# A decode kernel (sliding-window attention beside a SwiGLU block): SyncE's wait for the output put behind the block, two loads put ahead of the branches into it

## The chip, the cores and the metric

The kernel runs on one core of a Trainium2 chip. Its time is the device time of one execution in microseconds (us); the figure used is the median of several executions. The core has five engines: TensorE (PE, with its weight loads shown as PEld), VectorE (DVE), ScalarE (ACT), GpSimd (POOL) and SyncE (SP), which computes nothing and issues transfers here. Each engine works through its own list of instructions, in order. They meet only at semaphores: an instruction can wait until a semaphore has reached a value, and can raise one when it is done. A transfer (DMA) is issued by an engine, is then carried out by 16 DMA engines that all queues share, and raises its semaphore by 16 when it has landed.

## What is computed

The reference, cut to what matters (B = 4, one query token, D = 512, 32 query heads on 8 key heads, Dh = 128, a window W of the last 4096 of 16384 cached keys, F = 1792; all bf16):

```python
x = A_x
xn = layernorm(x)
q = (xn @ wq)                                  # per head
k, v = k_cache[:, :, Sk - W:], v_cache[:, :, Sk - W:]
scores = einsum("bhqd,bhkd->bhqk", q, k) * Dh ** -0.5
o = einsum("bhqk,bhkd->bhqd", softmax(scores), v)
ffn = (silu(xn @ w_gate) * (xn @ w_up)) @ w_down
return x + o.reshape(B, 1, Hq * Dh) @ wo + ffn
```

## The kernel before

The kernel is written engine by engine inside one `nc.Block()` (L171): five functions, one for each engine, are the lists of instructions that the engines branch into when the block begins. The order on every engine is the one written there; no planner moves anything. When the block ends, all engines go through a barrier: each drains and raises a common semaphore, POOL collects the four others and then releases all of them. These instructions carry the block's line, L171. A barrier of the same kind stands ahead of the kernel's first instruction and carries L500, the line at which the program is made.

SP issues all the large loads, in one queue: W_Q (L231), the first two blocks of K (`load_k`, L217), W_gate and W_up (L234, L235), then by turns a block of V (`load_v`, L221) and a block of K, 16 of each in all, then W_down (L240), the last block of V in halves (L225) and W_O in four groups of 16, 10, 4 and 2 of its 32 parts (L229; `WO_CUTS`, L120). K and V have two buffers each. Before a K block is issued, SP waits for the transposes that read the buffer's former content (`s_tr`), and before a V block for the products that read the V buffer (`s_pv`). Last, SP waits for the result y (L246), issues its first half to memory (L247) and waits until both halves have landed (L248: `d_out` at 32, 16 for each half). That wait rides on SP's branch out of the block.

ACT issues the load of x (L252), which has a queue of its own, and at the end the other half of y (L267). Between them it computes: the layer norm's steps (L254 to L260), an exponential for each block of scores (L263), and one for the gate (L265). ACT does not wait for its half of the output; SP's wait covers it.

The layer norm goes from DVE (L272, the row sum, which waits for x) over ACT (L254 to L260) and PE (L359, four small transposes) back to DVE (L279, which writes xnT). PE then waits for W_Q and multiplies (L354, called from L369). In the loop over the 16 blocks, PE transposes K (L382), DVE copies the transposes out of PSUM (L294), and PE forms scores and the products with V (L354). Behind the loop come the gate and up products, the last V block, W_down, and last the products with W_O, each group of which waits for its load (L483). The product's end lets DVE copy y out of PSUM (L349), and this releases both output transfers.

POOL fills constants at the start (L175 to L210) and then goes to the block's end.

Of the kernel before, what the change touches and what calls it, by code (L numbers as in the profile page):

```python
# [10 lines left out]
def bass_parallel_sum__sliding_block_cached__swiglu_ffn__decode_kernel(  # L11
# [10 lines left out]
    out: bass.AP,  # L22
):
    B, _, D = A_x.shape
    _, HKV, Sk, Dh = A_k_cache.shape
    HQ = A_wq.shape[1] // Dh
    F = B_w_gate.shape[1]
# [25 lines left out]
    WQ = sb("wq_sb", [128, NC * HQ * Dh], BF16)  # L53
# [18 lines left out]
    X = sb("x_sb", [B, D], BF16)  # L72
# [39 lines left out]
    def sem(name):  # L112
        return nc.alloc_semaphore(name=name)
    d_x = sem("d_x")
    d_wq = sem("d_wq")
# [3 lines left out]
    d_out = sem("d_out")  # L119
# [38 lines left out]
    x_ap = A_x.rearrange("b s d -> (b s) d")  # L158
    out_ap = out.rearrange("b s (n c) -> n (b s) c", n=2)
    wq_ap = A_wq.rearrange("(p c) n -> p (c n)", c=NC)  # L160
# [6 lines left out]
    def kv_ap(cache, d):  # L167
        b0 = d % 2 * 2
        return cache[b0:b0 + 2, d // 2, Sk - W:, :].rearrange("b (q t) d -> q b (t d)", t=NT)

    with nc.Block() as block:  # L171

        @block.gpsimd
# [38 lines left out]
        @block.sync  # L212
        def _(eng):
            def load_k(d):
                if d >= 2:
                    eng.wait_ge(s_tr, 2 * NG * (d - 1))
                eng.dma_start(KB[:, d % 2 * KVN:(d % 2 + 1) * KVN], kv_ap(A_k_cache, d)).then_inc(d_k[d % 2], 16)  # L217

            def load_v(d):
                eng.wait_ge(s_pv, d + 1)  # L220
                eng.dma_start(VB[:, d % 2 * KVN:(d % 2 + 1) * KVN], kv_ap(A_v_cache, d)).then_inc(d_v[d % 2], 16)  # L221

            def load_v_half(d, h, done):
                a = d % 2 * KVN + h * HKN
                eng.dma_start(VB[:, a:a + HKN], kv_ap(A_v_cache, d)[:, :, h * HKN:(h + 1) * HKN]).then_inc(done, 16)  # L225

            def load_wo(n):
                a, b = WO_CUTS[n], WO_CUTS[n + 1]
                eng.dma_start(WO[:, a:b, :], wo_ap[:, a:b, :]).then_inc(d_wo[n], 16)  # L229

            eng.dma_start(WQ[:], wq_ap).then_inc(d_wq, 16)  # L231
            load_k(0)
            load_k(1)
            eng.dma_start(WG[:], wg_ap).then_inc(d_wg, 16)  # L234
            eng.dma_start(WU[:], wu_ap).then_inc(d_wu, 16)  # L235
            load_v(0)
            for d in range(2, ND):
                load_k(d)
                load_v(d - 1)
            eng.dma_start(WD[:], wd_ap).then_inc(d_wd, 16)  # L240
            eng.wait_ge(s_pv, ND)
            load_v_half(ND - 1, 0, d_v[1])
            load_v_half(ND - 1, 1, d_vz)
            for n in range(len(d_wo)):
                load_wo(n)
            eng.wait_ge(s_y, 1)  # L246
            eng.dma_start(out_ap[0], y[0:B, :]).then_inc(d_out, 16)  # L247
            eng.wait_ge(d_out, 32)  # L248

        @block.scalar  # L250
        def _(eng):
            eng.dma_start(X[:], x_ap).then_inc(d_x, 16)  # L252
            eng.wait_ge(s_xc, 1)
            eng.activation(xc[:], X[:], ACT.Identity, bias=st_neg[:, 0:1], scale=float(D))  # L254
            eng.drain()
            eng.activation(xsq[:], xc[:], ACT.Square, accum_out=st_sum[:, 0:1]).then_inc(s_ss, 1)
            eng.wait_ge(s_var, 1)
            eng.activation(st_std[:], st_var[:], ACT.Sqrt).then_inc(s_std, 1)
            eng.wait_ge(s_rs, 1)
            eng.activation(xn[:], xc[:], ACT.Identity, scale=st_rstd[:, 0:1]).then_inc(s_xn, 1)  # L260
            for d in range(-1, ND):
                eng.wait_ge(s_sh, d + 2)
                eng.activation(P[:, d % 2 * PS:d % 2 * PS + SN], ps_S[d % 2][:], ACT.Exp, scale=SCALE).then_inc(s_p, 1)  # L263
            eng.wait_ge(s_gt, 1)
            eng.activation(ex[:], gT.rearrange("p (t b) -> p t b", b=32)[:, :, 0:B], ACT.Exp, scale=-1.0).then_inc(s_ex, 1)  # L265
            eng.wait_ge(s_y, 1)
            eng.dma_start(out_ap[1], y[64:64 + B, :]).then_inc(d_out, 16)  # L267
# [218 lines left out]
            last.then_inc(s_acc, 1)  # L486


# [1 line left out]
_INS = ['A_x', 'A_k_cache', 'A_v_cache', 'A_wq', 'A_wo', 'B_x', 'B_w_gate', 'B_w_up', 'B_w_down']  # L490
_OUTS = [((4, 1, 512), 'bfloat16')]
# [23 lines left out]
```

## Time and profile before

| | |
|---|---|
| three runs | 197.1, 197.37 and 197.96 us; median 197.37 |
| the profiled execution, its own time | 196.87 us |
| its span, first to last instruction | 195.1 us |
| granted TensorE clock, mean | 0.991 |
| busy | PE 83%, PEld 72%, DVE 59%, ACT 9%, POOL 5% of the span |
| moved | 81.10 MB, mean 416 GB/s |

The span is what the profile shows, from the first instruction of any engine to the last. The device time is longer by what lies before and behind it. In the profile's lines, a name with a q (SPq, ACTq) is an engine's sequencer: register, branch, drain, semaphore and DMA-issuing instructions, which are not counted as busy. A line of the timeline gives start, duration, engine, line, operation, and in brackets how long the engine had been idle and what ended it. A line of a source view gives the engine, the operation, its count, the shortest, median and longest duration in ns, and the start of the first and the last. A line of the waits gives total, count and longest. A line of the table by stages gives the stage, its length, each engine's busy time with its number of instructions, the granted clock, the DMA engines' busy share and what they moved.

### The profile page before, as it was taken

What the parts mean: (1) busy time and instruction counts of PE and PEld (TensorE: products, weight loads), DVE (VectorE), ACT (ScalarE), POOL (GpSimd) and SP (SyncE); (2) the same over time, 40 slices, a digit from 0 to 9 for tenths busy, and PEclk for the clock granted to TensorE, in tenths of its full rate; (3) what the DMA queues carried; (4) which work ended last, traced back from release to release, by engine and by line L of the source; (5) the groups of instructions that cost most, each with busy time, mean ns of one, the idle gap of its engine ahead of it and who ended that gap; (6) DMA issues with size and microseconds to landing.
All of it is one profiled execution on the core that took longest, in us unless ns stands there. A gap on an engine that the chain in (4) does not pass through costs nothing.

```text
span 195.1 us, 7758 instructions
## 1 busy us (share of the span) xinstructions
PE 162.7 (83%) x3466; PEld 140.2 (72%) x3467; DVE 114.9 (59%) x250; ACT 16.6 (9%) x26; POOL 10.3 (5%) x23
## 2 busy tenths in 40 slices
PE   0127999379898989898989898989898989898995
PEld 0113898368887888788878787878787878786752
DVE  1005777237676767676767676767676767675610
ACT  5600101001010101010101010101010101010000
POOL 8930000000000000000000000000000000000000
PEclk9999999789999999999999999999999999999999
DMA  6999999999999999999999999999999999999991
GB/s 222 430 430 430 432 420 437 421 430 430 430 433 430 433 433 430 433 430 433 433 437 430 430 430 430 430 430 430 430 430 430 430 433 433 430 428 420 438 407 68
DMA packets 5934, 81.10 MB, mean 416 GB/s; under 512 B 668, under 2 KB 680, under 8 KB 936
## 3 DMA queue, kind: packets, MB, share of 16 engines
q1 hardware_dynamic: 5912, 81.01, 97.4%
q8 instruction: 5, 0.08, 0.1%
q10 hardware_dynamic: 16, 0.01, 0.0%
q14 instruction: 1, 0.01, 0.0%
HBM read 81.01 MB, written 0.00 MB: 415 GB/s over the span
## 4 chain that ended last, share of the span: by engine, by line
DMA 63%; PE 32%; issue 1%; DVE 1%; SPq 1%; DVEq 0%
DMA kbuf<-in_A_k_cache_dram 48%; PE ps_kt L382 16%; DMA wo_sb<-in_A_wo_dram 9%; PE ps_s L354 8%; DMA wq_sb<-in_A_wq_dram 6%; PE ps_o L354 5%; PE ps_acc L354 2%; PE ps_kt L354 2%; DVE kT L294 1%; SPq L225 1%; DVE kT L282 0%; SPq L229 0%; DVE y_sb L349 0%; DVE qz L285 0%; DVEq L293 0%
## 5 line engine op out<-in xcount | busy, mean ns | idle before, releaser
L294 DVE COPY kT<-ps_kt 128x1024 bf16<-128x1024 bf16 x128 | 79.5, 683 | 25.3 <-PE ps_kt L382 25.3
L382 PE MATMUL ps_kt<-ident,kbuf 128*128 128x128 bf16 x1024 | 62.8, 219 | 10.6 <-DMA kbuf<-in_A_k_cache_dram 10.6
L382 PEld LDWEIGHTS ps_kt<-ident,kbuf 128*128 128x128 bf16 x1024 | 57.3, 98 | 15.8 <-issue 15.7
L354 PE MATMUL ps_o<-p,vbuf 128*128 128x64 bf16 x1120 | 39.2, 195 | 0.0
L354 PEld LDWEIGHTS ps_o<-p,vbuf 128*128 128x128 bf16 x1120 | 36.0, 99 | 1.1
L354 PEld LDWEIGHTS ps_s<-qz,kT 128*128 128x128 bf16 x1024 | 31.7, 98 | 6.7 <-issue 3.6
L354 PE MATMUL ps_s<-qz,kT 128*128 x1024 | 34.9, 192 | 1.3
L299 DVE TENSOR_REDUCE rm<-ps_s 128x8 bf16<-128x512 f32 x17 | 11.8, 692 | 23.7 <-PE ps_s L354 23.7
L263 ACT ACTIVATE p<-ps_s 128x512 bf16<-128x512 f32 x17 | 10.1, 597 | 162.1 <-PE ps_s L354 162.1
L354 PE MATMUL ps_o<-p,ones 128*128 128x128 bf16 (+1 forms) x69 | 7.1, 225 | 4.6 <-DMA vbuf<-in_A_v_cache_dram 3.2
L354 PEld LDWEIGHTS ps_o<-p,ones 128*128 128x128 bf16 x69 | 4.6, 100 | 5.6 <-DMA vbuf<-in_A_v_cache_dram 3.4
L354 PE MATMUL ps_kt<-wq_sb,xnT 128*32 128x512 bf16 x32 | 3.4, 610 | 5.2 <-DMA wq_sb<-in_A_wq_dram 5.2
L359 PE MATMUL ps_acc<-i,xn 4*128 4x4 f32 x4 | 0.6, 254 | 7.4 <-ACT xn L260 7.4
L354 PE MATMUL ps_s<-mkc,mkr 2*128 2x512 bf16 x17 | 6.5, 385 | 0.0
L354 PE MATMUL ps_s<-dg,ones 8*128 8x512 bf16 x17 | 6.5, 385 | 0.0
L354 PEld LDWEIGHTS ps_kt<-wq_sb,xnT 128*32 128x32 bf16 x32 | 1.3, 140 | 6.8 <-issue 6.8
L282 DVE STREAM_TRANSPOSE kT<-ps_kt 128x512 f32<-128x512 f32 x2 | 1.4, 718 | 7.8 <-PE ps_kt L354 7.8
L359 PEld LDWEIGHTS ps_acc<-i,xn 4*128 4x128 f32 x4 | 0.6, 207 | 7.3 <-issue 7.3
L310 DVE TENSOR_REDUCE den<-ps_o 128x8 f32<-128x128 f32 x18 | 4.9, 274 | 1.0 <-PE ps_o L354 1.0
L207 POOL MEMSET vbuf<- 128x6144 f32 x1 | 5.2, 5222 | 0.0
L304 DVE TENSOR_REDUCE m<-ps_acc 8x1 f32<-8x128 f32 x17 | 4.6, 269 | 0.3 <-PE ps_acc L354 0.3
L314 DVE TENSOR_TENSOR oT<-ps_o,den 128x8 f32 (+1 forms) x18 | 3.0, 167 | 2.9 <-issue 2.7
(67 smaller groups left out, 50.0 us busy)
## 6 DMA issues: line engine op xcount, KB each, us to landing
kbuf<-in_A_k_cache_dram SPq DMA_DIRECT2D x16, 2048.0 KB, 12.6
vbuf<-in_A_v_cache_dram SPq DMA_DIRECT2D x15, 2048.0 KB, 11.3
wq_sb<-in_A_wq_dram SPq DMA_DIRECT2D x1, 4096.0 KB, 12.3
vbuf<-in_A_v_cache_dram SPq DMA_DIRECT2D x2, 1024.0 KB, 9.2
wo_sb<-in_A_wo_dram SPq DMA_DIRECT2D x1, 2048.0 KB, 14.4
wg_sb<-in_B_w_gate_dram SPq DMA_DIRECT2D x1, 1792.0 KB, 25.7
wu_sb<-in_B_w_up_dram SPq DMA_DIRECT2D x1, 1792.0 KB, 29.3
wd_sb<-in_B_w_down_dram SPq DMA_DIRECT2D x1, 1792.0 KB, 15.0
```

The costliest lines, as they stand in the source:

```text
L207: eng.memset(VB[:, HKN:].bitcast(FP32), 0.0)
L225: eng.dma_start(VB[:, a:a + HKN], kv_ap(A_v_cache, d)[:, :, h * HKN:(h + 1) * HKN]).then_inc(done, 16)
L263: eng.activation(P[:, d % 2 * PS:d % 2 * PS + SN], ps_S[d % 2][:], ACT.Exp, scale=SCALE).then_inc(s_p, 1)
L282: eng.transpose(qT[:, 512 * n:512 * n + 512], ps_kt[n][:])
L294: eng.tensor_copy(KT[:, u * HKN + 1024 * g:u * HKN + 1024 * (g + 1)], kt_ps[g].rearrange("p a b -> p (a b)")).then_inc(s_ev, 1)
L299: eng.tensor_reduce(RM[:], ps_S[bank][:].rearrange("p (t c) -> p c t", c=C), AX.X, ALU.max).then_inc(s_rm, 1)
L304: eng.tensor_reduce(m8[:], mt_ps, AX.X, ALU.max)
L310: eng.tensor_reduce(den[:], den_ps.rearrange("p (t c) -> p c t", c=C), AX.X, ALU.add)
L314: eng.tensor_tensor(OT[:, 2 * b:2 * b + 2, ds(r * REP, REP)], O_ps.rearrange("p (j h) -> p j h", j=2), den[:].rearrange("p (j h) -> p j h" ...
L354: return eng.matmul(o, l, r, start=start, stop=stop, skip_group_check=True)
L359: last = eng.transpose(xT_ps[:, c * B:(c + 1) * B], xn[:].rearrange("b (p c) -> b c p", c=NC)[:, c, :], I4[:])
L382: last = eng.transpose(kt_ps[g][:, k, :], KB[:, a:a + 128], ident[:])
```

## The change

The wait for the output leaves SP's function and stands behind the block, where SP executes it after the barrier. The issues of W_Q (on SP) and of x (on ACT) leave their functions and stand ahead of the block, between the start barrier and the branches. Nothing else differs; every later line of the kernel moves by some lines, so that the wait is on L490, the issues on L172 and L173, and the block on L175.

```diff
+    nc.sync.dma_start(WQ[:], wq_ap).then_inc(d_wq, 16)
+    nc.scalar.dma_start(X[:], x_ap).then_inc(d_x, 16)
+
     with nc.Block() as block:
...
-            eng.dma_start(WQ[:], wq_ap).then_inc(d_wq, 16)
             load_k(0)
             load_k(1)
...
             eng.wait_ge(s_y, 1)
             eng.dma_start(out_ap[0], y[0:B, :]).then_inc(d_out, 16)
-            eng.wait_ge(d_out, 32)
 
         @block.scalar
         def _(eng):
-            eng.dma_start(X[:], x_ap).then_inc(d_x, 16)
             eng.wait_ge(s_xc, 1)
...
             last.then_inc(s_acc, 1)
 
 
+    nc.sync.wait_ge(d_out, 32)
```

In the built program, each engine's instructions stand in the same order as before but for these three; PE's, DVE's and POOL's lists are the same.

## The prediction

> **What bounds the kernel now.** I read the page's head, its 40 slices, the queues and the chain of waits first.
>
> ```profile
> span 195.1 us, 7758 instructions
> ...
> DMA  6999999999999999999999999999999999999991
> ...
> q1 hardware_dynamic: 5912, 81.01, 97.4%
> q8 instruction: 5, 0.08, 0.1%
> q10 hardware_dynamic: 16, 0.01, 0.0%
> q14 instruction: 1, 0.01, 0.0%
> ...
> DMA 63%; PE 32%; issue 1%; DVE 1%; SPq 1%; DVEq 0%
> ```
>
> The 16 DMA engines are busy in every slice but the first and the last, and SP's queue q1 alone fills 97.4% of them. The table by stages says how dense that stream is in the middle and how it ends.
>
> ```profile
> core 0: us, PE busy (x) PEld busy (x) DVE busy (x) ACT busy (x) POOL busy (x), PEclk, DMA share, GB/s
> 0.00:1.85 1.85, 0.00 (x0) 0.00 (x0) 0.00 (x0) 0.45 (x1) 1.26 (x12) 1.00 0.01 2
> ...
> 100.00:185.00 85.00, 77.91 (x1746) 68.92 (x1748) 57.82 (x127) 5.62 (x10) 0.00 (x0) 1.00 1.01 431
> ...
> 190.00:192.20 2.20, 2.07 (x29) 1.10 (x29) 0.00 (x0) 0.00 (x0) 0.00 (x0) 1.00 0.50 193
> 192.20:193.40 1.20, 0.68 (x10) 0.09 (x4) 0.43 (x1) 0.00 (x0) 0.00 (x0) 1.00 0.00 0
> 193.40:195.10 1.70, 0.00 (x0) 0.00 (x0) 0.00 (x0) 0.00 (x0) 0.00 (x0) 1.00 0.01 2
> ```
>
> DMA share 1.01 in the long stage: the loads run without a gap, at 431 GB/s. The change can thus matter in two places only: ahead of the stream (the first 1.85 us move next to nothing) and behind it (from 192.2 us on DMA share is 0.00 to 0.01). I read those two ends instruction by instruction. First the start: the chain of waits in order of time, SP's start barrier, and the timeline.
>
> ```profile
> 0.73 0.07 issue
> 0.80 12.29 DMA wq_sb<-in_A_wq_dram
> ```
> ```profile
> L500 SPq EVENT_SEMAPHORE  x1: 17/17/17, 0.7 to 0.7; - x1
> ```
> ```profile
> 0.80 0.41 SPq L231 DMA_DIRECT2D wq_sb<-in_A_wq_dram  x1
> 0.81 0.56 ACTq L252 DMA_DIRECT2D x_sb<-in_A_x_dram  x1
> ...
> 1.27 1.34 SPq L217 DMA_DIRECT2D kbuf<-in_A_k_cache_dram  x2
> ...
> 1.41 1.28 ACT L254 ACT_TABLE_LOAD   x1 [1.41 <-PEq L500]
> ...
> 2.56 0.67 DVE L272 TENSOR_REDUCE st_neg<-x_sb 4x1 f32<-4x512 bf16 x1 [2.56 <-DMA x_sb<-in_A_x_dram]
> ...
> 8.02 0.17 DVE L279 CAST xnT<-ps_acc 128x16 bf16<-128x16 f32 x1 [1.55 <-PE ps_acc L359]
> ```
>
> SP leaves the start barrier at 0.73 us, and 0.07 us later W_Q is issued: that gap holds the branch into SP's block. The end, from the timeline, the waits of SP's queue, and the instructions of the block's own line, L171:
>
> ```profile
> 192.49 0.09 PEld L354 LDWEIGHTS ps_acc<-wo_sb,oP 128*4 128x4 bf16 x4 [0.29 <-DMA wo_sb<-in_A_wo_dram]
> 192.92 0.43 DVE L349 CAST y_sb<-ps_acc 128x256 bf16<-128x256 f32 x1 [5.54 <-PE ps_acc L354]
> 193.37 0.35 SPq L247 DMA_DIRECT2D out_dram<-y_sb  x1
> 193.38 0.28 ACTq L267 DMA_DIRECT2D out_dram<-y_sb  x1
> ```
> ```profile
> SPq L171 <- DMA out_dram<-y_sb: 1.0, 1, 1.0
> ```
> ```profile
> L171 POOLq EVENT_SEMAPHORE  x2: 17/17/17, 195.0 to 195.0; - x2
> L171 POOLq DRAIN  x1: 89/89/89, 11.4 to 11.4; - x1
> L171 PEldq DRAIN  x1: 432/432/432, 192.5 to 192.5; - x1
> L171 DVEq DRAIN  x1: 458/458/458, 192.9 to 192.9; - x1
> L171 ACTq DRAIN  x1: 241/241/241, 193.7 to 193.7; - x1
> L171 SPq COMPARE_BRANCH  x1: 33/33/33, 194.8 to 194.8; - x1
> L171 SPq DRAIN  x1: 13/13/13, 194.9 to 194.9; - x1
> L171 SPq EVENT_SEMAPHORE  x1: 17/17/17, 195.1 to 195.1; - x1
> ...
> L171 DVEq EVENT_SEMAPHORE  x1: 21/21/21, 195.1 to 195.1; - x1
> L171 PEldq EVENT_SEMAPHORE  x1: 51/51/51, 195.1 to 195.1; - x1
> ```
>
> The last group of W_O ends PE's wait, the copy of y follows, both halves of the output are issued, and SP waits 1.0 us for them. Only then come SP's branch (194.8), its drain (194.9), POOL's two semaphore steps (195.0) and the release (195.1): the barrier that closes the block stands wholly behind the landing of the output.
>
> **The change part by part, the end.** SP's wait moves behind the barrier. SP's issue ends at 193.37 + 0.35 = 193.72; its branch and drain take about what they take now from 194.8 to 194.9, some 0.15 us, so SP arrives at about 193.9. ACT's drain ends at 193.7 + 0.24 = 193.9, DVE's at 193.4, PE's at 192.9, POOL's long before. From SP's drain to the release are 0.2 us now (194.9 to 195.1), so the release falls at 193.9 + 0.2 = 194.1. The output lands as before, at 193.72 + 1.0, about 194.75, since its issue and everything ahead of it is untouched. So the barrier is covered by the flight of the output with 194.75 - 194.1 = 0.6 us to spare, and if that cover were gone it would cost its 0.3 us again. Nothing is queued behind the moved wait on SP, and no engine waits for it. What is left behind the landing is one semaphore step of 17 ns. Saved: 195.1 less 194.75, with the rounding of the rows 0.3 to 0.4 us; I take 0.35.
>
> **Outside the span.** The profiled execution took 196.87 us and its span is 195.1, so 1.77 us lie around it, which no row divides. In the changed kernel four engines leave the barrier at 194.1, not 195.1, and may do their share of what follows while SP still waits: between nothing (SP, released last, has the longest way left) and the 0.6 us of that head start. I take 0.1, near the lower bound, because SP's own share still stands behind the landing. The Trainium skill, "Runtime: NRT & Kernel Launch", section "The ~15µs preamble/postamble breakdown", puts a barrier that waits for all engines right behind a kernel; by it alone the head start is worth nothing, and this term would be 0.0. No view of this trace reaches there.
>
> **The start.** W_Q's issue on SP and x's issue on ACT now precede the branches. Of the 0.07 us gap the branch can be anything from nothing to all; SP's closing branch took 33 ns and its next instruction came some 0.1 us after, so most of the gap is the branch, and I take 0.05. W_Q was the first entry of SP's queue and x of ACT's, so neither is moved past another transfer; each remains one issue, of 0.41 and 0.56 us. What comes after, on SP the issue of the first two K blocks and on ACT the table load, gets the branch in front instead and starts at 1.27 and 1.41 as now. That costs nothing: W_Q's 4096 KB, 4.19 MB, keep the queues busy for 4.19 / 431 = 9.7 us, so the K blocks could be issued 9 us later before the stream had a gap. The 0.05 us of the earlier stream pass to the end, since there is no gap in it and PE at 192.49 waits for its last load. x earlier by 0.05 gains nothing: its chain ends with xnT at 8.02 + 0.17 = 8.2 and W_Q lands at 13.09, 4.9 us later; for the same reason x could even land that much later at no cost.
>
> **Sum.** 0.35 + 0.1 + 0.05 = 0.5 us. Against the profiled execution that is 196.87 - 0.5 = 196.37; that execution was 0.5 below the median of the three runs shown (197.1 to 197.96), and it is the median that the next runs are to be set beside: 197.37 - 0.5 = 196.87, so 196.9. Bounds of the terms: 0.3 + 0 + 0 = 0.3 and 0.4 + 0.6 + 0.07 = 1.07.
>
> **Rivals.** *The head start counts in full.* If the share of the 1.77 us that ends last belongs to another engine than SP, the gain is the upper sum, 1.07: 197.37 - 1.07 = 196.3. For it: PE and DVE leave with longer release steps, 51 and 21 ns, than SP's 17. Against: SP is the one that leaves last. Chance 0.2.
>
> *The change doesn't do what it says.* If a drain held its engine until that engine's transfers had landed, SP's would wait for the output inside the barrier, and only the branch's 0.05 would be left: 197.3. Against it, plainly: ACT's drain ended at 193.9 with ACT's own half of the output still in flight until about 194.75. Chance 0.1, which also holds the case that a new step behind the landing eats the gain.
>
> *Slower: the branch has to fetch.* If SP's branch needs its block's instructions from memory, the fetch now stands behind a 4 MB load rather than ahead of it. Place: SP between W_Q and the first K block. It decides once the stall outlasts the load, that is over 9 us; then the stream has a gap of one short transfer, issue to use, as x shows it (0.81 to 2.56): 1.75 us. Time: 197.37 - 0.45 + 1.75 = 198.7. Against it: the present branch fits in 0.07 us, which leaves no room for a fetch; the page counts just six instruction packets in the whole span; and x, in another queue than W_Q's, came through in 1.75 us, not 9. The Trainium skill speaks for this rival ("Runtime: NRT & Kernel Launch", "Instruction fetch mechanics": a taken branch whose target isn't in the instruction memory has to fetch it by DMA); the 0.07 us says that this target was there. Chance 0.04.
>
> *Slower: the stream ends raggedly.* In 190.0 to 192.2 DMA share is 0.50: the 16 engines don't finish together, and half of 2.2 us, 1.1, is lost there. A start shifted by 0.05 could hand the instruction packets, or x, to other engines at other moments and spread the finish wider; it decides once the last engine is over 0.45 us later than now, and at 1.1 later the time is 197.37 - 0.45 + 1.1 = 198.0. Against: order and sizes of all loads stay. Chance 0.06.
>
> **How the numbers follow.** Forecast, a gain of 0.3 to 0.7 (196.7 to 197.1): 0.6; the rivals 0.2, 0.1, 0.04 and 0.06. This kernel's runs, 0.86 us apart, let about 0.5% be told from no change, here 1.0 us: faster means below 196.4, slower above 198.4. Faster: the first rival and, by the scatter of the runs, a part of the forecast, 0.26. Slower: the fetch and a tail at its worst, 0.06. Within: 0.68. The range takes in the upper sum with half of the runs' scatter below it, 196.3 - 0.4 = 195.9, and the ragged finish above, 198.0.
>
> **What would show it.** In the changed profile: SP's issue of W_Q at about 0.75 with K still near 1.27; the block's POOL semaphore steps at about 194.05 and the releases at 194.1; one SP semaphore instruction on the new last line that starts at about 194.7 after a wait on the output; a span of 194.7 (195.1 - 0.4). If the releases stand behind the landing, the drain waits for transfers. If the span falls by 0.4 but the time by 1.0, the head start counts. If K's first issue is microseconds late, the branch fetches. A stage at the end with DMA share well under 0.50 over a longer stretch is the ragged finish. I would be wrong altogether if the span grew.

## The result, and the profile after

| | before | changed |
|---|---|---|
| median of 8 runs each | 197.45 us | 196.34 us |
| ratio, 95% interval | | 0.9949 (0.9933 to 0.9965) |
| profiled execution, its own time | 196.87 us | 195.96 us |
| its span | 195.1 us | 194.7 us |
| time less span, profiled execution | 1.77 us | 1.26 us |

The change took 1.1 us off the median, 0.5% of the time; the interval of the ratio stands for 0.7 to 1.3 us. Of the 0.91 us between the two profiled executions, the span gave 0.4, and what lies outside the span gave 0.5 (with the spans to the nanosecond, 195.145 and 194.720, it is 0.43 and 0.48). One run in all that follows, 309.95 us of the kernel called *pool late* below, counts as slow and is left out of that kernel's figures. The stream of loads, which bounds the kernel, is what it was, as the changed kernel's table by stages shows:

```profile
100.00:185.00 85.00, 77.98 (x1746) 68.97 (x1748) 57.77 (x127) 5.62 (x10) 0.00 (x0) 1.00 1.01 431
185.00:190.00 5.00, 4.79 (x61) 2.86 (x57) 0.85 (x2) 0.00 (x0) 0.00 (x0) 1.00 0.96 400
190.00:192.20 2.20, 2.12 (x31) 1.09 (x29) 0.00 (x0) 0.00 (x0) 0.00 (x0) 1.00 0.51 200
```

DMA share 1.01 at 431 GB/s through the long stage, and 0.51 in the ragged last 2.2 us, against 0.50 before. The start of the changed kernel, from its timeline:

```profile
0.80 0.56 ACTq L173 DMA_DIRECT2D x_sb<-in_A_x_dram  x1
0.80 0.41 SPq L172 DMA_DIRECT2D wq_sb<-in_A_wq_dram  x1
...
1.26 1.30 SPq L221 DMA_DIRECT2D kbuf<-in_A_k_cache_dram  x2
...
1.40 1.28 ACT L255 ACT_TABLE_LOAD   x1 [1.40 <-PEq L504]
```

W_Q is issued at 0.80, as it was when a branch stood in front of it, and K and the table load, which now have the branch in front of them, are within 0.01 of 1.27 and 1.41. No cost of the branch can be seen on either side. Now the end: the timeline, the waits of SP's queue, the block's own line (now L175), and the line of the moved wait.

```profile
192.43 0.09 PEld L355 LDWEIGHTS ps_acc<-wo_sb,oP 128*4 128x4 bf16 x4 [0.29 <-DMA wo_sb<-in_A_wo_dram]
192.86 0.43 DVE L350 CAST y_sb<-ps_acc 128x256 bf16<-128x256 f32 x1 [5.54 <-PE ps_acc L355]
193.31 0.35 SPq L250 DMA_DIRECT2D out_dram<-y_sb  x1
```
```profile
SPq L490 <- DMA out_dram<-y_sb: 0.6, 1, 0.6
SPq L175 <- PEq L175: 0.2, 1, 0.2
```
```profile
L175 POOLq EVENT_SEMAPHORE  x2: 17/17/17, 193.9 to 194.0; - x2
...
L175 ACTq DRAIN  x1: 241/241/241, 193.6 to 193.6; - x1
L175 SPq DRAIN  x1: 168/168/168, 193.7 to 193.7; - x1
L175 SPq EVENT_SEMAPHORE  x1: 17/17/17, 194.0 to 194.0; - x1
L175 ACTq EVENT_SEMAPHORE  x1: 17/17/17, 194.0 to 194.0; - x1
L175 DVEq EVENT_SEMAPHORE  x1: 21/21/21, 194.0 to 194.0; - x1
L175 PEldq EVENT_SEMAPHORE  x1: 51/51/51, 194.0 to 194.0; - x1
```
```profile
L490 SPq EVENT_SEMAPHORE  x1: 17/17/17, 194.7 to 194.7; - x1
```

The last loads, the copy of y and the output's issue come 0.06 us earlier than in the trace of before, which is within what two runs of one kernel differ by. The barrier, which before stood from 194.8 to 195.1 behind the output's landing, now runs at 193.9 to 194.0. SP's wait on the output fell from 1.0 to 0.6 us, the rest of the flight being spent in the barrier, and one step of 17 ns at 194.7 is all that is left of the span behind the landing.

The 0.5 us outside the span are in no view of instructions. The trace also records the time of each update of a semaphore, and near the end one semaphore is updated in small steps that no instruction of the kernel makes. They come in two rounds of nine, which I read as five on the way in and four on the way back; behind the first round most other semaphores are updated once more (from 195.81 to 196.48 us in the trace of before). The times in us of the first five steps and of the last of the second round, with the landing of the output (the last update of `d_out`):

```
                    output landed   steps 1 to 5                                  last step of all
before                    194.744   195.384  195.419  195.625  195.669  195.693   197.064
changed                   194.686   194.332  194.366  194.573  194.617  194.837   196.144
```

In the changed kernel four of the five steps are made before the output has landed, and the fifth, 0.117 us after SP's last instruction (ended at 194.720), follows the landing by 0.15 us; before, it followed by 0.95. That is 0.80 us less, and what comes after the fifth step is 0.06 shorter too (the step that follows the fifth comes 0.04 us later in the changed kernel and 0.11 before). With the 0.06 by which the output landed earlier, these make 0.92; the two profiled executions differ by 0.91. That the medians differ by more, 1.11, is within the interval.

### The profile page after: what moved, and what is told of

The parts are those of the page before. It is cut to its first block, busy times and chain, and to the rows that moved or that the text cites. A ratio compares the mean times of both kernels' runs of the same rounds, so it can differ in the third digit from the quotient of the medians.

```text
span 194.7 us, 7758 instructions
## 1 busy us (share of the span) xinstructions
PE 161.6 (83%) x3466; PEld 138.9 (71%) x3467; DVE 114.9 (59%) x250; ACT 16.6 (9%) x26; POOL 10.3 (5%) x23
## 4 chain that ended last, share of the span: by engine, by line
DMA 62%; PE 32%; issue 2%; DVE 1%; SPq 1%; DVEq 0%
DMA kbuf<-in_A_k_cache_dram 47%; PE ps_kt L383 16%; DMA wo_sb<-in_A_wo_dram 9%; PE ps_s L355 8%; DMA wq_sb<-in_A_wq_dram 6%; PE ps_o L355 5%; PE ps_acc L355 2%; PE ps_kt L355 2%; DVE kT L295 1%; SPq L229 1%; DVE kT L283 0%; SPq L233 0%; DVE y_sb L350 0%; DVE qz L286 0%; DVEq L294 0%
## 5 line engine op out<-in xcount | busy, mean ns | idle before, releaser
L355 PE MATMUL ps_o<-p,vbuf 128*128 128x64 bf16 x1120 | 38.4, 193 | 0.0
L355 PEld LDWEIGHTS ps_o<-p,vbuf 128*128 128x128 bf16 x1120 | 35.2, 98 | 1.1
```

The source lines that it names most:

```text
L355: return eng.matmul(o, l, r, start=start, stop=stop, skip_group_check=True)
```

## The experiments

The theory after the result: behind the kernel's own instructions the five engines check in one after another; SP is the last of them; before the change the first could not start until the block's barrier had released them, and that stood behind the landing. With the wait on SP alone, the four others check in while the output is still in flight. The rival: any share of work by the freed engines, in no order, so that it matters only that four are free. In all runs the time less the span tells more than the ratio: it is within about 0.1 us of its median in every run (before: 1.69 to 1.87 in 31 runs), while the span scatters by about 1 us. There are three sessions; each kernel's ratio is to the kernel before in its own session.

**One half of the change at a time.** The wait alone:

```diff
-            eng.wait_ge(d_out, 32)
...
+    nc.sync.wait_ge(d_out, 32)
```

> Only the wait is moved behind the block; the loads stay inside. Chain theory (behind the span the engines check in one after another, SP last, and with the wait on SP alone the four others check in while the output is in flight): the whole gain, span about 194.7, time less span about 1.25, ratio to before about 0.995. Rival that the early loads carry part of it (0.05 to 0.2 us through an earlier stream): a ratio nearer 0.996 and W_Q's issue later than 0.80.

The loads alone (the other hunks of the change):

> Only the loads are issued ahead of the branches; the wait stays inside the block. Chain theory: nothing, ratio 1.000 within 0.002, span about 195.1, time less span about 1.77, W_Q issued at 0.80 as before. Rival that the early loads matter: W_Q issued at about 0.75 and the ratio 0.9995 or lower, down to 0.999.

The wait alone gave a ratio of 0.9954 (0.9937 to 0.9971) and time less span 1.25 us: the whole effect, as far as these runs can tell. The loads alone gave 0.9984 (0.9969 to 0.9999), medians of 197.09 and 197.17 us, and time less span 1.73 against 1.76 of the kernel before in the same session. Its timeline, and SP's wait at the end:

```profile
0.80 0.41 SPq L172 DMA_DIRECT2D wq_sb<-in_A_wq_dram  x1
0.81 0.56 ACTq L173 DMA_DIRECT2D x_sb<-in_A_x_dram  x1
```
```profile
SPq L175 <- DMA out_dram<-y_sb: 1.0, 1, 1.0
```

The issue is not earlier at all, and W_Q is issued at 0.80 in the kernel with the wait alone as well. The interval just misses 1, but the trace holds nothing that could be the cause, and 0.08 us of the medians is a tenth of the runs' scatter; I take it for no effect, which is argued and not shown.

**Another engine waits.** In the changed kernel the last line is put on another engine, or on all five:

```diff
-    nc.sync.wait_ge(d_out, 32)
+    nc.tensor.wait_ge(d_out, 32)
```

> As the changed kernel, but PE and not SP waits for the output behind the block. Chain theory: SP checks in early and PE late; whoever stands behind PE in the chain waits for it. If PE stands first, time less span goes back to about 1.7 (ratio about 0.998); if in the middle, 1.3 to 1.6. Rival (any four free engines do their share in parallel, no order): time less span stays at 1.25 and the ratio at 0.995. The span is about 194.75 either way.

> As the changed kernel, but ACT and not SP waits for the output behind the block. Chain theory: time less span lies above 1.25, up to about 1.7 if ACT stands first in the chain, and differs from that with PE waiting, since they can't both be at the same place. Rival (no order): 1.25 as with SP, ratio 0.995. The span is about 194.7 either way.

> As the changed kernel, but DVE waits for the output behind the block. Chain theory: time less span above 1.25, up to 1.7, at a place of its own between the other engines'. Rival (no order): 1.25, ratio 0.995.

> As the changed kernel, but POOL waits for the output behind the block. Chain theory: time less span above 1.25, up to 1.7, at a place of its own. Rival (no order): 1.25, ratio 0.995.

> All five engines wait for the output behind the block, so the block's barrier is still covered by the output's flight but no engine has a head start. Chain theory: the span falls by the barrier's 0.35 to about 194.75, time less span stays at about 1.7, ratio about 0.998. Rival (the time outside the span follows something else in the change): time less span 1.25, ratio 0.995.

| who waits behind the block | time less span, median (least to most) | ratio | steps 1 to 5, us after the landing |
|---|---|---|---|
| nobody (before; wait in the block) | 1.76 (1.69 to 1.87) | | 0.64, 0.67, 0.88, 0.92, 0.95 |
| SP (the change) | 1.24 (1.20 to 1.28) | 0.9949 (0.9933 to 0.9965) | -0.35, -0.32, -0.11, -0.07, 0.15 |
| DVE | 1.38 (1.34 to 1.41) | 0.9963 (0.9951 to 0.9975) | -0.32, -0.29, -0.11, 0.20, 0.23 |
| ACT | 1.44 (1.37 to 1.49) | 0.9962 (0.9944 to 0.998) | -0.32, 0.15, 0.19, 0.24, 0.26 |
| PE | 1.57 (1.50 to 1.66) | 0.9991 (0.997 to 1.0012) | 0.28, 0.31, 0.35, 0.39, 0.42 |
| POOL | 1.83 (1.78 to 1.93) | 0.9993 (0.9983 to 1.0002) | -0.36, -0.32, 0.58, 0.62, 0.65 |
| all five | 1.72 (1.71 to 1.79) | 0.9993 (0.9976 to 1.001) | 0.28, 0.31, 0.58, 0.62, 0.65 |

In the other two sessions the first row's median is 1.74 and 1.73. The ratios alone can't put these engines in order, since their intervals overlap; the order rests on the two other columns. Time less span counts from the last instruction, which ends 0.40 us after the landing in the first row and 0.03 to 0.08 in the others; the last column counts from the landing itself.

The last column says which step is whose: with PE waiting the first step comes late, with ACT the second, with POOL the third, with DVE the fourth, with SP the fifth, and every later step follows the late one. So the order is PE, ACT, POOL, DVE, SP, and the rival without an order falls: it had 1.25 for each. PE did not come out at the 1.7 expected of the first place but at 1.57. The column shows a second thing that the theory did not have. A late engine checks in 0.11 or 0.12 us after its last instruction if it is ACT or SP, 0.16 if DVE, 0.20 if PE, but 0.54 if it is POOL: its wait ended at 195.001 us in its run, and the third step came at 195.539.

```profile
L490 POOLq EVENT_SEMAPHORE  x1: 17/17/17, 195.0 to 195.0; - x1
```

Where POOL is not late, the third step still comes 0.57 us after POOL's last instruction, before the change (195.058 to 195.625) and after it (194.006 to 194.573). POOL's slow step is why the wait on the third engine costs more than on the first: with PE waiting, POOL's 0.57 us run under the output's flight. It is also why what lies outside the span is as long in the kernel before as with all five waiting. The ratio for PE, 0.9991, is worse than its 1.57 would make it: its median span, 195.6 us, lay 0.3 to 0.45 over those of the other kernels in its group. I take that for the scatter of the spans, whose least, 194.8, is like the others'; no run shows it.

With all five waiting, the span is 195.05 in median against 195.4 of the kernel before in that session: the barrier is covered there too and nothing else is, which is the span's share of the gain by itself. The ratio, whose interval takes in 1, is too coarse to show it.

**How much cover there is.** The block's barrier is held back by a memset on POOL, which waits for y and clears a buffer that is no longer read; the wait on the output stays on SP, as in the change. Shown is the longer memset (*pool later*); the short one (*pool late*) clears `VB[:, 0:1580]`.

```diff
             eng.engine_nop().then_inc(d_v[1], 16)
+            eng.wait_ge(s_y, 1)
+            eng.memset(VB[:, 0:2160].bitcast(FP32), 0.0)
```

> The changed kernel with a memset of 128x790 f32 on POOL that waits for y and then holds the block's barrier back by about 0.2 us (it clears a buffer that nothing reads any more). Theory of the chain with POOL's slow check-in as its longest step: the releases come at about 194.25, the fourth check-in at about 194.8, as SP's, so nothing is lost: span 194.7 and time less span 1.25. Rival (the cover is gone as soon as anything is later): 1.45.

> The same with a memset of 128x1080 f32, which holds the barrier back by about 0.45 us. The prediction's cover of 0.6 us, which counts only to the release, says nothing is lost: span 194.7, time less span 1.25. The chain theory says the span stays, as the releases at 194.5 are still ahead of the landing, but the fourth check-in, 0.6 after the release, comes at about 195.05, 0.2 behind SP's, and time less span is 1.45 to 1.5.

> The changed kernel again, beside the two. Span 194.7 to 195.2, time less span 1.24, ratio 0.995.

The longer memset in the timeline of its run, and the barrier behind it:

```profile
193.77 0.35 SPq L252 DMA_DIRECT2D out_dram<-y_sb  x1
...
193.80 1.00 POOL L216 MEMSET vbuf<- 128x1080 f32 x1 [182.49 <-DVE y_sb L352]
```
```profile
L175 POOLq EVENT_SEMAPHORE  x2: 17/17/17, 194.9 to 195.0; - x2
...
L175 SPq EVENT_SEMAPHORE  x1: 17/17/17, 195.0 to 195.0; - x1
```
```profile
L492 SPq EVENT_SEMAPHORE  x1: 17/17/17, 195.2 to 195.2; - x1
```

Counted from the copy of y, the barrier came 0.28 us later than in the changed kernel with the short memset and 0.53 with the long one, more than I had aimed at. The release at 195.0 is still ahead of the landing (SP's wait ends at 195.2), so the span stays covered, as expected of both. But time less span rose to 1.43 (1.39 to 1.44) with the short and to 1.69 (1.62 to 1.73) with the long memset, against 1.24 (1.21 to 1.29) of the changed kernel beside them. The ratios are 0.9975 (0.9956 to 0.9995), 0.998 (0.996 to 0.9999) and 0.9955 (0.9935 to 0.9974).

The short memset did not come out at the 1.25 expected by the theory, but near the 1.45 of the rival, that the cover is gone as soon as anything is later. The steps decide between them.

The spare time is that of the fourth step, not of the release: 194.837 less 194.617, 0.22 us, in the changed kernel, of which 0.02 is the way from the fourth step to the fifth. A barrier late by 0.28 should then push the fifth step back by about 0.08 (0.28 less the 0.20 that is left), one late by 0.53 by 0.33; by the rival it would go back by 0.28 and 0.53. The fifth step followed the landing by 0.244 and 0.483 us against 0.151: 0.09 and 0.33 later. So about 0.2 us were to spare, as the theory has it, and the cover of 0.6 us that my prediction counted is not there. Time less span rose by somewhat more than the fifth step: as between before and changed, the time behind the fifth step is some 0.06 longer when the steps come in one row. That accounts for all of it in the profiled executions, whose spans are known to the nanosecond (195.034, 195.181 and 195.893 us of the changed kernel): there time less span is 1.41 and 1.64 against 1.25, so 0.16 and 0.39 more. The medians' 0.19 and 0.45 are from spans rounded to 0.1 us.

## Why the prediction was right or wrong

The range and the direction held; the likeliest time, 196.9, was 0.5 us too high, and the most likely class, within 0.5%, was missed by a hair: the ratio is 0.9949 with an interval on both sides of 0.995. The terms as the traces have them, 0.4 in the span, 0.5 outside and nothing at the start, make 0.9: nearer to the upper sum, the rival that I had called *the head start counts in full* at a chance of 0.2, than to my 0.5. That its 196.3 was met to within 0.04 us is luck in part: its 1.07 held 0.07 at the start that is not there and 0.6 outside where 0.5 was, and the medians differ by 0.2 more than the traced parts.

- **The end within the span**, 0.35 us from bounds of 0.3 to 0.4: right. The profiled spans differ by 0.4, with 0.06 of it from a slightly earlier landing, and in the sessions of the experiments the median span fell from 195.4 to between 194.9 and 195.2 in most kernels with a wait behind the block. Each step of it is in the profile: releases at 194.0 (194.1 predicted), SP's last instruction at 194.7, a span of 194.7.
- **Outside the span**, 0.1 us from bounds of 0 to 0.6: this is the step that failed. It measured 0.5 (1.76 to 1.24). I had chosen the lower end because SP's own share still stands behind the landing. It does, but that share is 0.12 us; the long share is POOL's 0.57, behind which DVE and SP check in, and it went under the output's flight. So SP is the last to check in, as I had argued, and yet not what took the time. The upper bound, the 0.6 us from release to landing, came near in size by luck: what is gained is the way from the barrier to the fifth step, 0.59 us after SP's last instruction before and 0.12 now, and the flight only had to be long enough to cover it. The rival's own reason, the longer release steps of PE and DVE, is not the cause either. The trace of before already holds the semaphore updates and shows 0.95 us between the landing and the fifth step; the prediction went by the views of instructions and left the 1.77 us undivided.
- **The rule of the Trainium skill** weighed there ("Runtime: NRT & Kernel Launch", "The ~15µs preamble/postamble breakdown": a barrier behind the kernel waits for all engines) would have made this term nothing by itself. The trace agrees that such a barrier is there, but it takes the engines one after another, so it does matter which one comes late: 1.24 us with SP, 1.83 with POOL.
- **The start**, 0.05 us from bounds of 0 to 0.07: wrong, it is 0.00. I put the gap of 0.07 between the barrier and the first issue down to the branch. The same gap is there without a branch, so it belongs to the issue; and no trace records a branch there: those recorded stand in the loops of DVE and PE and, before the change, at SP's end, where it carried the wait. x came to DVE at 2.39 and not 2.56, which is scatter (2.26 with the wait alone moved, 2.89 in a later trace of the changed kernel); nothing gained by it, as predicted.
- **The rivals.** That a drain would hold its engine until its transfers have landed is out: SP's drain ended at 193.9, 0.8 us ahead of the landing. That the branch would have to fetch is out: K is issued at 1.26. The ragged finish did not move: DMA share 0.51 against 0.50.
- **The cover**, 0.6 us to spare until the barrier would cost again: true of the span and false of the time, which has about 0.2.

The chance given to the upper sum, 0.2, was too low for a term whose bounds were 0 and 0.6 and which I had not divided; I let one argument on SP pick the end, where the argument said nothing of the other four engines.

## What to carry to other kernels

In a kernel that ends like this one, a wait that only guards the end belongs behind the closing barrier, and on the engine that is last to check in there (here SP), so that the barrier and the other engines' way out run while the last transfer flies. With the same line on POOL the fifth step follows the landing by 0.65 us, against 0.15 with SP and 0.95 before, and the ratio, 0.9993, can't be told from 1. A gap in front of an instruction is not yet the cost of the branch that stands there: here the same 0.07 us was left without it. Compare the time less the span as well as the span: half of this gain stood outside the span.

## What the runs showed of the hardware

- Behind the kernel the engines check in as PE, ACT, POOL, DVE, SP, 0.02 to 0.04 us from step to step when those behind have long been free (with PE waiting: 195.001, 195.036, 195.075, 195.119 and 195.142 us).
- POOL's check-in comes 0.54 us after its last instruction when POOL is the late one (195.001 to 195.539 us), SP's and ACT's 0.12 and 0.11 when they are (194.720 to 194.837 and 194.836 to 194.949 us).
- With 512-byte rows, an output of 2 KB in each of two queues lands 1.37 us after its issue begins (193.372 to 194.744 us).
